# Turning all outputs back on VectorE, and issuing SyncE's transfers in program order

## The chip, the cores and the metric

The kernel runs on one core of a Trainium2 chip. The metric is the device time of one execution in microseconds, as the median of several runs. The core has five engines that run their own instruction streams in order: PE (TensorE, matrix multiply), DVE (VectorE), ACT (ScalarE), POOL (GpSimd) and SP (SyncE, which here only starts transfers). They wait for each other through semaphores.

## The reference, cut to what matters

Two blocks follow each other. The first is attention where each row keeps only its 32 highest scores; the second mixes along the sequence with a low-rank matrix and then runs a two-layer network over the channels.

```python
def _attn_ref(q, k, v):                      # (8, 8, 576, 64) each
    top_k = 32
    scores = scale * np.matmul(q, k.transpose(0, 1, 3, 2))
    kth = np.partition(scores, -top_k, axis=-1)[..., -top_k:-top_k + 1]
    scores = np.where(scores >= kth, scores, -1000000000.0)
    scores = scores - np.max(scores, axis=-1, keepdims=True)
    attn = np.exp(scores)
    attn = attn / (np.sum(attn, axis=-1, keepdims=True) + 1e-09)
    return np.matmul(attn, v)

def _moe_ref(x, U, V, w_ch1, w_ch2):         # x: (8, 576, 512); rank 32; 512 -> 2048 -> 512
    h = x.transpose(0, 2, 1) @ U @ V
    u = x + h.transpose(0, 2, 1)
    ch = np.maximum(u @ w_ch1, 0.0) @ w_ch2
    return u + ch
```

## The kernel before

The work is cut into 32 pairs of heads (four pairs to a batch) and each pair into five row chunks `t`: four of 128 rows, for both heads, and one of 64 rows of both heads together. One row chunk is one step. DVE finds the top 32 of each row with MAX8 and MATCH_REPLACE8, four and three times per head.

PE, ACT, DVE and POOL run their instructions in the order in which the program states them; SP's order is left to the scheduler:

```python
ctx.enter_context(tc.manual_schedule(engines={PE, ACT, DVE, POOL}))
```

PE needs the softmax weights transposed. For head 1 of a chunk, DVE turns 32x32 blocks (`y`), SP writes them to HBM (`away`) and reads them back rearranged (`PT`); this is what `blocks` does. PE multiplies `PT` with v a step later, in `values`:

```python
def blocks(g, t):
    ...
    y = attn.tile([P, 4, NT, BLK], F32, tag="y", name="y", bufs=1)
    nc.vector.transpose(y..., E2[:, S + TAIL : 2 * S]...)
    away = dram.tile([P, 4, P], F32, tag="away", name="away")
    for a in range(4):
        nc.sync.dma_start(away[:, a]..., y[a * BLK : (a + 1) * BLK]...)
    nc.sync.dma_start(PT[:, NT : 2 * NT]..., away...)
```

`load(g)` starts the transfers of a pair: for pairs 5 and later 16 for q and k into one buffer `ld`, and five for v into one of three sets of buffers (`va`, `vd`, `vt`). DVE then turns `ld` into `qkT`. While a batch's attention runs, the network of the batch before it is fed to PE in small portions (`fill`), eight times in a step. It works on transposed activations, with 320 and then 256 of the 576 rows at a time. Its result `oT` is therefore transposed and is turned back, in four blocks of 128 channels for each of the two row groups:

```python
def mlp(b):
    ...
    for chunks, (lo, hi) in zip(PARTS, SPAN):        # 320 rows, then 256 rows
        w = hi - lo
        ...                                          # first layer: 16 x 4 matmuls, Relu on ACT
                if f == 3 and late:
                    late.pop()()
        for c in range(NC):
            po = ps_m.tile([P, C], F32, tag="mm", name="mm")
            for f in range(NF):
                nc.tensor.matmul(po[:, 0:w], lhsT=w2[...], rhs=hTs[f][:, 0:w], ...)
                if f == 9 and late:
                    late.pop()()
                if f < NF - 1:
                    yield w / C
            oT = mlpp.tile([P, WIDE], F32, tag="oT", name="oT")
            if b == B - 1:
                nc.vector.tensor_tensor(oT[:, 0:w], uT[:, c, lo:hi], po[:, 0:w], ALU.add)
            else:
                nc.scalar.copy(oT[:, 0:w], po[:, 0:w])
                nc.gpsimd.tensor_tensor(oT[:, 0:w], oT[:, 0:w], uT[:, c, lo:hi], ALU.add)
            late.append(turned_back(b, chunks, lo, c, oT))
            yield w / C
    late.pop()()
```

So a block is turned back ten matmuls into the next block, except the last one of a batch, which is turned back at once. There are two ways to do it. The last batch goes through DVE in 32x32 blocks, with transfers that put the blocks in place; the others go through PE, PSUM and ACT:

```python
def turned_back(b, chunks, lo, c, oT):
    def run():
        cs = slice(c * P, (c + 1) * P)
        if b == B - 1 and (lo, c) != (SPAN[1][0], NC - 1):
            w = sum(rows(t) for t in chunks)
            ob = mlpp.tile([P, 3 * P], F32, tag="ob", name="ob", bufs=2)
            nc.vector.transpose(ob[:, 0:w], oT[:, 0:w])                       # L631
            for a in range(4):
                ...
                for t in chunks[0:2]:
                    nc.sync.dma_start(out[...], ba[...])                      # L636
                if NT in chunks:
                    nc.sync.dma_start(out[...], ba[...])                      # L641
            return
        tp = ps_t.tile([P, 3, P], F32, tag="tp", name="tp")
        for i, t in enumerate(chunks):
            nc.tensor.transpose(tp[...], oT[...], ident)                      # L649
        ob = mlpp.tile([P, 3, P], F32, tag="ob", name="ob", bufs=2)
        nc.scalar.copy(ob[:, 0:2], tp[:, 0:2, :])                             # L651
        if NT in chunks:
            nc.scalar.copy(ob[0:TAIL, 2], tp[0:TAIL, 2, :])                   # L653
        nc.sync.dma_start(out[...], ob[:, 0:2])                               # L655
        if NT in chunks:
            nc.sync.dma_start(out[...], ob[0:TAIL, 2])                        # L660
    return run
```

## Time and profile before

| | |
|---|---|
| time, median of 3 runs | 1765.89 us (1764.58 to 1766.87) |
| span of the profiled run | 1765.1 us |
| transposes of oT on PE (L649) | 142, own duration 273 ns (median) |
| copies to ob on ACT (L651, L653) | 57 of 373 ns and 28 of 259 ns |
| transposes of oT on DVE (L631) | 7 of 483 ns (mean) |
| transfers of results, SP (L655, L660) | 57 and 28 |
| transfers of results, SP (L636, L641) | 56 and 16 |
| time in which the 16 DMA engines moved q1's packets | 26.0% |

A line number such as L631 names the line of the kernel that made an instruction. Names such as `oT` or `PT<-away` are those of the program's buffers, written as output<-input. PEld is the load of a matmul's stationary operand. "Busy" of PE is the time covered by its records; the records of neighbouring matmuls overlap, so an instruction's own duration is not what it adds. In "A <- B" A is the waiting instruction and B the one that released it; SPq is SP's queue of transfers.

### The profile page before, as it was taken

What the parts mean: (1) busy time and instruction counts of PE and PEld (TensorE: products, weight loads), DVE (VectorE), ACT (ScalarE), POOL (GpSimd) and SP (SyncE); (2) the same over time, 40 slices, a digit from 0 to 9 for tenths busy, and PEclk for the clock granted to TensorE, in tenths of its full rate; (3) what the DMA queues carried; (4) which work ended last, traced back from release to release, by engine and by line L of the source; (5) the groups of instructions that cost most, each with busy time, mean ns of one, the idle gap of its engine ahead of it and who ended that gap; (6) DMA issues with size and microseconds to landing.
All of it is one profiled execution on the core that took longest, in us unless ns stands there. A gap on an engine that the chain in (4) does not pass through costs nothing.

```text
span 1765.1 us, 28989 instructions
## 1 busy us (share of the span) xinstructions
PE 1670.0 (95%) x9851; PEld 1259.5 (71%) x9851; DVE 1540.3 (87%) x3106; ACT 1026.2 (58%) x2682; POOL 846.4 (48%) x591
## 2 busy tenths in 40 slices
PE   4576889999999999999999999999999999999999
PEld 2444556777777877788777877788777877788677
DVE  7999989999999999999999999999999999994000
ACT  4778787655655665565656556565656656564100
POOL 4777677445545454444444454545354554543000
PEclk7677799999999999999999999999999999999999
DMA  3232232232223332222223232223233232211010
GB/s 99 84 90 72 81 85 61 51 66 70 66 59 76 72 72 64 67 66 66 61 62 81 66 72 63 70 61 70 58 68 80 64 76 56 56 45 45 4 15 13
DMA packets 275829, 112.79 MB, mean 64 GB/s; under 512 B 173920, under 2 KB 260192, under 8 KB 275680
## 3 DMA queue, kind: packets, MB, share of 16 engines
q1 hardware_dynamic: 274624, 110.68, 26.0%
q8 instruction: 77, 1.26, 0.3%
q14 instruction: 72, 0.59, 0.1%
q10 hardware_dynamic: 1056, 0.26, 0.1%
HBM read 74.15 MB, written 36.70 MB: 63 GB/s over the span
## 4 chain that ended last, share of the span: by engine, by line
PE 78%; DVE 13%; POOL 4%; ACT 3%; issue 1%; DMA 1%; SPq 0%; POOLq 0%; DVEq 0%
PE mm L582 26%; PE mm L601 25%; PE sc L333 7%; PE O L513 6%; DVE rr L396 6%; DVE m L400 5%; PE tp L475 3%; DVE first L385 2%; PE sc L320 2%; PE O L499 2%; PE up L557 1%; PE O L509 1%; POOL E L403 1%; PE up L559 1%; PE tp L649 1%
## 5 line engine op out<-in xcount | busy, mean ns | idle before, releaser
L400 DVE MAX8 m<-rr 128x8 f32<-128x576 f32 x864 | 614.3, 747 | 5.5
L601 PE MATMUL mm<-hT,w 128*128 128x256 f32 (+1 forms) x2048 | 547.4, 410 | 0.0
L582 PE MATMUL mm<-uT,w 128*128 128x256 f32 (+1 forms) x2048 | 541.1, 410 | 0.8 <-ACT hT L594 0.8
L403 POOL TENSOR_SCALAR E<-Ssb,m 128x576 f32<-128x576 f32 x127 | 280.9, 2212 | 366.2 <-DVE m L400 346.1
L582 PEld LDWEIGHTS mm<-uT,w 128*128 128x128 f32 x2048 | 371.7, 190 | 114.7 <-issue 26.0
L601 PEld LDWEIGHTS mm<-hT,w 128*128 128x128 f32 x2048 | 368.5, 190 | 106.6 <-issue 22.5
L396 DVE MATCH_REPLACE8 rr<-m,rr 128x576 f32<-128x576 f32 x576 | 423.2, 741 | 0.0
L422 POOL TENSOR_TENSOR Ssb<-Ssb,E 128x576 f32<-128x576 f32 x159 | 224.8, 1414 | 147.6 <-ACT E L421 147.6
L594 ACT ACTIVATE hT<-mm 128x320 f32<-128x320 f32 (+1 forms) x256 | 105.0, 410 | 243.8 <-PE mm L582 243.3
L351 ACT ACTIVATE E<-Ssb,nmax 128x576 f32<-128x576 f32 x288 | 223.0, 776 | 37.3 <-POOL Ssb L404 28.1
L385 DVE MAX8 first<-Ssb 128x8 f32<-128x576 f32 x288 | 203.7, 743 | 38.5 <-ACT Ssb L346 37.8
L396 DVE MATCH_REPLACE8 rr<-first,Ssb 128x576 f32<-128x576 f32 x288 | 211.7, 742 | 0.0
L404 POOL TENSOR_TENSOR Ssb<-Ssb,E 128x576 f32<-128x576 f32 x127 | 179.1, 1410 | 10.6
L333 PE MATMUL sc<-qkT 64*128 64x288 f32 x1024 | 170.7, 454 | 6.3 <-ACT Ssb L344 5.2
L513 PE MATMUL O<-PT,va 128*64 128x128 f32 x2048 | 145.4, 285 | 2.0 <-DMA PT<-away 2.0
L475 PE MATMUL tp<-ident,E 128*128 128x128 f32 x736 | 116.0, 284 | 31.5 <-ACT XT L522 11.6
L476 ACT COPY PT<-tp 128x512 f32<-128x512 f32 x184 | 106.4, 585 | 58.0 <-PE tp L475 55.4
L475 PEld LDWEIGHTS tp<-ident,E 128*128 128x128 f32 x736 | 92.5, 146 | 63.2 <-ACT XT L522 13.4
L513 PEld LDWEIGHTS O<-PT,va 128*64 128x64 f32 x2048 | 113.6, 140 | 18.5 <-DMA PT<-away 2.2
L421 ACT ACTIVATE E<-Ssb,least 128x576 f32<-128x576 f32 x159 | 123.3, 776 | 5.2
L333 PEld LDWEIGHTS sc<-qkT 64*128 64x128 f32 x1024 | 93.2, 197 | 44.6 <-issue 14.0
L614 DVE TENSOR_TENSOR oT<-uT,mm 128x320 f32<-128x320 f32 (+1 forms) x8 | 3.6, 454 | 137.1 <-PE mm L601 137.1
(81 smaller groups left out, 1576.4 us busy)
## 6 DMA issues: line engine op xcount, KB each, us to landing
away<-y SPq DMA_DIRECT2D x416, 64.0 KB, 1.8
PT<-away SPq DMA_DIRECT2D x104, 256.0 KB, 2.7
raw<-in_moe_w_ch_dram SPq DMA_DIRECT2D x32, 512.0 KB, 3.8
va<-in_v_dram SPq DMA_DIRECT2D x64, 128.0 KB, 2.2
out_dram<-ob SPq DMA_DIRECT2D x57, 128.0 KB, 2.1
ld<-in_q_dram SPq DMA_DIRECT2D x108, 64.0 KB, 2.4
ld<-in_k_dram SPq DMA_DIRECT2D x108, 64.0 KB, 2.3
ld<-in_q_dram SPq DMA_DIRECT2D x108, 8.0 KB, 2.1
```

Source lines behind the costliest of these rows:

```text
L333: nc.tensor.matmul(sc[:, h, 0:HALF], lhsT=qkT[half(h), 0, cols(t)], rhs=qkT[half(h), 1, i * HALF : (i + 1) * HALF], start=True, stop=True,)
L351: nc.scalar.activation(E, chunk, AF.Exp, bias=nmax, scale=SCALE, accum_out=total)
L385: nc.vector.max(ms[c], curs[c])
L396: nc.vector.match_replace(nxt, ms[c], curs[c], NEG)
L400: nc.vector.max(ms[c], curs[c])
L403: nc.gpsimd.tensor_scalar(Es[c], chunks[c], ms[c][:, 7:8], NEG, ALU.is_lt, ALU.mult)
L404: nc.gpsimd.tensor_tensor(chunks[c], chunks[c], Es[c], ALU.add)
L422: nc.gpsimd.tensor_tensor(chunks[c], chunks[c], Es[c], ALU.subtract)
L475: nc.tensor.transpose(tp[:, j, :], E2[:, a : a + P], ident)
L513: nc.tensor.matmul(O[half(h)], lhsT=va[:, h, j, :], rhs=PB[:, j] if h and shared(g, t) else PT[:, NT * h + j], start=False, stop=(j == NT ...
L582: nc.tensor.matmul(ph[:, 0:w], lhsT=w1[:, cc, f * P : (f + 1) * P], rhs=uT[:, cc, lo:hi], start=(cc == 0), stop=(cc == NC - 1),)
L601: nc.tensor.matmul(po[:, 0:w], lhsT=w2[:, f, c * P : (c + 1) * P], rhs=hTs[f][:, 0:w], start=(f == 0), stop=(f == NF - 1),)
```

## The change

The results of all batches but for one block of the last take the way through DVE, which frees PE and ACT of that work. With it come many more and smaller transfers (eight or twelve in place of one or two per block), and SP is put under the program's order as well, so that its transfers are issued as the program states them.

```diff
-    DVE, POOL = mybir.EngineType.DVE, mybir.EngineType.Pool
+    DVE, POOL, SP = mybir.EngineType.DVE, mybir.EngineType.Pool, mybir.EngineType.SP
...
-    ctx.enter_context(tc.manual_schedule(engines={PE, ACT, DVE, POOL}))
+    ctx.enter_context(tc.manual_schedule(engines={PE, ACT, DVE, POOL, SP}))
...
         def run():
             cs = slice(c * P, (c + 1) * P)
-            if b == B - 1 and (lo, c) != (SPAN[1][0], NC - 1):
+            if (b, lo, c) != (B - 1, SPAN[1][0], NC - 1):
 
                 w = sum(rows(t) for t in chunks)
                 ob = mlpp.tile([P, 3 * P], F32, tag="ob", name="ob", bufs=2)
```

## The prediction

> **What bounds the kernel now.** I read the page first, then the busy time by stretches, then the chain of work in one stretch, then who waited for whom. The engine totals look like two near-equal engines:

> ```profile
> PE 1670.0 (95%) x9851; PEld 1259.5 (71%) x9851; DVE 1540.3 (87%) x3106; ACT 1026.2 (58%) x2682; POOL 846.4 (48%) x591
> PE 78%; DVE 13%; POOL 4%; ACT 3%; issue 1%; DMA 1%; SPq 0%; POOLq 0%; DVEq 0%
> ```

> The second line, the shares of the chain that ended last, says PE. The busy time by stretches (columns: stretch, its length, then PE, PEld, DVE, ACT, POOL) says where:

> ```profile
> 400.00:450.00 50.00, 48.49 (x319) 38.11 (x317) 49.19 (x99) 30.03 (x81) 25.27 (x18) 1.00 0.30 71
> ...
> 700.00:750.00 50.00, 50.00 (x296) 35.89 (x292) 48.57 (x99) 28.10 (x76) 25.57 (x18) 1.00 0.29 70
> 750.00:800.00 50.00, 50.00 (x324) 41.07 (x324) 47.63 (x96) 31.32 (x87) 22.63 (x15) 1.00 0.29 66
> ```

> Until about 440 us the vector engine sets the pace (49.2 of 50). From there PE never stops, but DVE is close behind (47.6 to 48.6 of 50), so there is little room to give it work. One pair of heads takes 50.0 us, a batch of four pairs 200.1 us. From 1616 us on only the last batch's MLP is left and DVE is nearly idle.

> What one transpose costs PE is read from the chain, not from its own duration (columns: start, us, what):

> ```profile
> 1115.44 0.33 PE tp L649 x3
> ...
> 1130.42 0.33 PE tp L649 x3
> ```

> Its own record is 273 ns, but the next matmul starts 0.11 us later. That is the price of a removed one. Last, the waits of SP and of PE (who, for whom, us, times, longest):

> ```profile
> SPq L453 <- DVE y L447: 333.3, 103, 13.9
> SPq L273 <- PE O L499: 117.1, 13, 9.4
> SPq L276 <- PE O L509: 114.7, 26, 12.4
> ...
> PE tp L649 <- POOL oT L617: 2.8, 2, 1.5
> ```

> SP sits at a transfer whose buffer PE has not freed (L273, L276: v fetched too early in the scheduler's order), but nobody suffers: PE waited only 2.0 us for PT<-away.

> [...] So the block grid must be undone by the transfers, and no PSUM copy is needed; the last batch does just that here (0.51 us for 128x320, 0.45 for 128x256). [...] 0.43 us to issue, 1.5 us to landing, for the last batch's output pieces. [...] The new pieces have 128 B; those of the last batch land in 1.5 us[...].

> **The change, part by part.** (1) PE loses the transposes of seven batches: per batch 4x3 + 4x2 = 20, so 140, at 0.11 us = 15.2 us. Of these 120 lie after 440 us, in the PE-bound part: 13.0 us. With them go PE's waits for POOL's oT, 2.8 us. Together 15.8 us gained.

> (2) ACT loses 56 copies of 0.37 and 28 of 0.26 us: 28 us, on an engine busy 58%. No gain of its own after 440 us.

> (3) DVE gets 56 transposes. Neighbours on DVE overlap by about 0.08 us (two MAX8 of 0.74 take 1.41), so they cost 0.43 and 0.37 us: 1.7 us in a pair of heads that emits four wide ones. DVE's 47.8 us of work per pair becomes 49.5, PE's 50.0 becomes about 49.5. Before 440 us DVE is the bound, and the eight transposes there cost 3.2 us nearly in full.

> (4) The DVE queue is in order, so its transpose waits in place for POOL's oT. The orders of both built kernels are the same on PE, DVE and POOL but for what is removed and inserted. So for each new transpose I take from the trace before when oT was ready and when DVE passed that place. In seven of eight per batch oT is ready 3 to 8 us earlier: no wait. The eighth, the last column block of a batch, is turned back at once, without the ten matmuls of delay the others have: oT was ready at 1040.18, DVE passed at 1035.64. DVE will stand 4.5 us there, in each of five steady batches, and 2.9 us in the first (before 440 us, where it counts in full).

> (5) What this costs PE. The stalled DVE is to make y 2.7 us later on, and y goes out to HBM and back as PT. Before: y ends 1039.05, four issues 1.76, landing 1.8, PT issued and landed 2.7, so about 1045.6 with the waits, and PE uses it at 1049.05. After: DVE resumes at 1040.2, the transpose ends 1040.6, y ends 1044.0; SP needs 8 x 0.47 = 3.8 us for the output pieces first and is free at 1044.5; then 1.8 + 1.8 + 0.4 + 2.7 gives 1051.1. PE stops 2 us. In the next step y comes at 1053.7 to 1054.4, PT at 1061.0, PE wants it (2 us late) at 1060.0: another 1 us. Then DVE's usual idle time at the one-chunk step (1.2 and 1.0 us) takes up the rest. Total 3 us per steady batch.

> (6) SP. In program order the 21 loads of the next pair (0.62 us each, 13 us) are issued in one block, with the output pieces behind: 12 x 0.47 = 5.6 us for a wide block, 3.8 for a narrow one, in place of one or two issues. In the pair with wide blocks SP has 13 + 4 x 4.2 + 22.6 = 52 us of work for 50 us, but the blocks lie over some 55 us. By hand, step after step, y finds SP busy for up to 2.4 us, and PT's margin of 1.5 to 4.4 us takes nearly all of it: 0.6 us of PE per batch. In the narrow pair (from about 810 us) the loads end at 824.6, the two blocks behind them at 832.2, while y is done at 828.1: PT lands 6.7 us after 832.2, at 838.9, and PE wants it at 838.6: about 0.5 us. The waits of L273 and L276 vanish, without gain.

> Sum: 1765.9 - 15.8 (PE) + 3.2 + 2.9 - 1 (before 440 us; the 1 is my guess for the freed ACT, whose copies lie in the chain there) + 5 x 3.0 (DVE's stall) + 6 x 0.6 + 5 x 0.5 (SP) = 1776. Several of these delays may hide behind each other, so I take **1773 us**, 0.4% slower.

> **Rivals.** *PE's relief comes through.* If the lead that DVE has over PE takes up the 4.5 us, all that is left is the gain: 1750 us, 0.9% faster. For it: PE waits almost nowhere before. Against: the margins of PT are 1.5 to 4.4 us, less than the delay. More than 1% cannot come of it, for PE has no other idle time to win. *SP becomes the bound.* If the output pieces take longer to issue or land among the other traffic than in the quiet tail, or the loads come too late for DVE's transpose into qkT (after the fourth wide block SP is free at 767.5; 16 loads of q and k take 10.4 us to issue and 2.4 to land, so 780.3, and DVE wants them at 780.30), each step loses one or two us: 8 us per batch, 1805 us or more. For it: SP is almost full in a wide pair. Against: the 16 DMA engines are busy 29% there. *DVE becomes the bound.* 47.8 + 0.8 on average + 1.1 (stall) + 0.4 of small gaps = 50.1 us per pair against 50.0: about 1769 us, the same as my number to the eye.

> **Range and chances.** The gain is bounded by 18 us; the losses are small delays that each could be double. So 1755 to 1800 us. Faster by over 2% would need 35 us that PE does not have: 0.02. Slower by over 2% needs SP's rival: 0.11. Within 2%: 0.87.

> **What will show it.** Right: PE's busy time about 38 us lower (140 x 0.27), but its share of steady stretches below 100%; a wait of DVE's L631 for oT L617, six times, about 4.5 us; waits of PE O L513 for PT<-away of some 20 us in all, up from 2.0; L636 and L641 issues of 0.43 us. Wrong if PE is again at 50.0 of 50 (then 1750), if L631 waits little, if qkT waits for a load, or if away and PT take over 1 us longer to land than 1.8 and 2.7 us.

## The result, and the profile after

The changed kernel takes **1792.32 us** (median of 4 runs, 1790.93 to 1793.99) beside 1766.38 us for the kernel before on the same chip (4 runs, 1764.58 to 1766.91). The ratio is **1.0149, with a 95% interval of 1.0131 to 1.0167**: 1.5% slower. The time lies in the predicted range of 1755 to 1800 us, 19 us above the predicted 1773.

The engine totals and the shares of the chain that ended last, of the kernel after:

```profile
PE 1665.0 (93%) x9711; PEld 1249.7 (70%) x9711; DVE 1560.3 (87%) x3162; ACT 1005.8 (56%) x2598; POOL 846.4 (47%) x591
PE 64%; DVE 19%; DMA 5%; SPq 5%; ACT 3%; POOL 3%; issue 2%; DVEq 0%; POOLq 0%
```

The totals hardly move: 140 PE instructions are gone and PE's busy time falls by 5 us only. The chain tells more: PE's share falls from 78 to 64%, and SP's queue, which had 0%, now holds 5%, with another 5% (before: 1%) for transfers under way.

The busy time by stretches (columns as before: stretch, its length, PE, PEld, DVE, ACT, POOL, then the clock that PE was granted, the share of DMA time, GB/s), after:

```profile
400.00:450.00 50.00, 48.20 (x299) 37.69 (x298) 46.46 (x97) 25.50 (x70) 22.86 (x17) 1.00 0.32 68
700.00:750.00 50.00, 50.00 (x295) 35.73 (x293) 48.67 (x101) 27.63 (x73) 24.95 (x17) 1.00 0.31 67
750.00:800.00 50.00, 48.97 (x301) 38.98 (x299) 48.35 (x98) 29.95 (x80) 23.24 (x15) 1.00 0.32 69
840.00:860.00 20.00, 17.83 (x97) 13.21 (x96) 17.26 (x35) 7.67 (x20) 10.50 (x8) 0.91 0.31 63
1000.00:1250.00 250.00, 245.12 (x1475) 188.59 (x1474) 236.05 (x480) 141.16 (x374) 115.50 (x78) 0.99 0.30 66
```

The same view of the kernel before, for the last stretch:

```profile
1000.00:1250.00 250.00, 249.76 (x1531) 192.82 (x1527) 238.83 (x481) 148.69 (x397) 121.24 (x82) 1.00 0.29 68
```

PE no longer fills the part that it bounded. The holes are local: none between 700 and 750 us, 1 us between 750 and 800, over 2 us in the 20 us from 840. DVE is not fuller either (236 of 250, before 239). So no engine has become the bound; something stands between them. The waits (who, for whom, us, times, longest) name it:

```profile
DVE ob L631 <- POOL oT L617: 41.1, 9, 10.5
PEld O L513 <- DMA PT<-away: 29.7, 21, 3.2
PE O L513 <- DMA PT<-away: 24.6, 18, 3.0
```

The last of these lines in the kernel before:

```profile
PE O L513 <- DMA PT<-away: 2.0, 1, 2.0
```

PE's wait for PT, the attention weights that travel to HBM and back, rises from 2.0 to 24.6 us. DVE's new transpose L631 waits for oT: six of these nine waits last 2.74 to 2.95 us and are the last column block of each batch; the other three, up to 10.5 us, are at the end of attention, where DVE has little else.

How such a stop of PE comes about can be followed around 845 us. First SP (start, us, what; a row with x16 is sixteen issues in a row, with the waits between them):

```profile
835.79 0.63 SPq L277 DMA_DIRECT2D vt<-in_v_dram  x1
836.53 8.89 SPq L636 DMA_DIRECT2D out_dram<-ob  x16
845.51 1.83 SPq L453 DMA_DIRECT2D away<-y  x4
848.80 0.34 SPq L457 DMA_DIRECT2D PT<-away  x1
849.23 7.58 SPq L636 DMA_DIRECT2D out_dram<-ob  x16
856.91 1.82 SPq L453 DMA_DIRECT2D away<-y  x4
```

Then DVE in the same microseconds (the bracket is the wait in front of a row):

```profile
838.18 0.69 DVE L447 STREAM_TRANSPOSE y<-E 128x512 f32<-128x512 f32 x1
...
850.05 0.45 DVE L631 STREAM_TRANSPOSE ob<-oT 128x256 f32<-128x256 f32 x1 [2.74 <-POOL oT L617]
...
853.17 0.69 DVE L447 STREAM_TRANSPOSE y<-E 128x512 f32<-128x512 f32 x1
```

And PE:

```profile
851.56 1.09 PE L513 MATMUL O<-PT,va 128*64 128x128 f32 x14 [2.17 <-DMA PT<-away]
852.58 1.88 PE L333 MATMUL sc<-qkT 64*128 64x288 f32 x8
854.39 3.97 PE L582 MATMUL mm<-uT,w 128*128 128x320 f32 x10
```

DVE finishes y at 838.87. SP is then two microseconds into sixteen output pieces, which in turn had stood behind 21 loads, and sends y at 845.51, 6.6 us later. PT is issued at 848.80 and lands at 851.5; PE stood from 849.39. The next y, ready at 853.86, waits until 856.91 behind the next sixteen pieces. Note also that DVE's own wait (847.3 to 850.05) comes after the late y: this stop is SP's, not DVE's.

The transfers themselves are no slower: `away`, PT and 16 KB pieces took a median of 1.8, 2.7 and 1.5 us from issue to landing before as well. The transfer part of the page of the kernel after (transfer, count, KB each, median us from issue to landing):

```profile
away<-y SPq DMA_DIRECT2D x416, 64.0 KB, 1.8
PT<-away SPq DMA_DIRECT2D x104, 256.0 KB, 2.7
...
out_dram<-ob SPq DMA_DIRECT2D x504, 16.0 KB, 1.5
```

### The profile page after: what moved, and what is told of

Its sections match the earlier page's. It is cut to its first block, busy times and chain, and to the rows that moved or that the text cites. A ratio compares the mean times of both kernels' runs of the same rounds, so it can differ in the third digit from the quotient of the medians.

```text
span 1789.1 us, 29116 instructions
## 1 busy us (share of the span) xinstructions
PE 1665.0 (93%) x9711; PEld 1249.7 (70%) x9711; DVE 1560.3 (87%) x3162; ACT 1005.8 (56%) x2598; POOL 846.4 (47%) x591
## 4 chain that ended last, share of the span: by engine, by line
PE 64%; DVE 19%; DMA 5%; SPq 5%; ACT 3%; POOL 3%; issue 2%; DVEq 0%; POOLq 0%
PE mm L582 24%; PE mm L601 19%; DVE rr L396 8%; DVE m L400 7%; PE sc L333 6%; PE O L513 5%; DVE first L385 3%; PE tp L475 3%; DMA PT<-away 2%; PE sc L320 2%; SPq L636 2%; PE O L499 1%; DMA away<-y 1%; PE up L557 1%; PE O L509 1%
## 5 line engine op out<-in xcount | busy, mean ns | idle before, releaser
L582 PE MATMUL mm<-uT,w 128*128 128x256 f32 (+1 forms) x2048 | 542.8, 412 | 2.4 <-ACT hT L594 2.4
L582 PEld LDWEIGHTS mm<-uT,w 128*128 128x128 f32 x2048 | 373.3, 191 | 120.0 <-issue 29.8
L333 PE MATMUL sc<-qkT 64*128 64x288 f32 x1024 | 170.9, 455 | 8.8 <-ACT Ssb L344 7.8
L513 PE MATMUL O<-PT,va 128*64 128x128 f32 x2048 | 154.9, 286 | 24.7 <-DMA PT<-away 24.6
L513 PEld LDWEIGHTS O<-PT,va 128*64 128x64 f32 x2048 | 118.1, 140 | 45.9 <-DMA PT<-away 29.7
L333 PEld LDWEIGHTS sc<-qkT 64*128 64x128 f32 x1024 | 93.4, 198 | 47.6 <-issue 15.5
```

The source lines that it names most:

```text
L333: nc.tensor.matmul(sc[:, h, 0:HALF], lhsT=qkT[half(h), 0, cols(t)], rhs=qkT[half(h), 1, i * HALF : (i + 1) * HALF], start=True, stop=True,)
L513: nc.tensor.matmul(O[half(h)], lhsT=va[:, h, j, :], rhs=PB[:, j] if h and shared(g, t) else PT[:, NT * h + j], start=False, stop=(j == NT ...
L582: nc.tensor.matmul(ph[:, 0:w], lhsT=w1[:, cc, f * P : (f + 1) * P], rhs=uT[:, cc, lo:hi], start=(cc == 0), stop=(cc == NC - 1),)
```

## The experiments

Two suspects: SP's queue in order (with 560 more output pieces in it, seven batches x 4 x (12 + 8), where the kernel before sent each block in one or two transfers), and DVE's wait in place for oT. Rivals: the program order on SP alone; the block of 21 loads; ACT's or DVE's changed load. All times are medians, and the ratios are to the kernel before on the same chip (1765.85 to 1766.4 us). "Stops" is PE's lost time between 440 and 1610 us, counted from the start times of the same matmuls in the trace before and in the trace of the run, with the time of the removed transposes taken out; it includes small shifts. In the kernel after it is 36.3 us. Stops and waits are those of the one profiled execution of each kernel. The pairs of heads in which blocks of 320 rows are turned are called wide below, those with blocks of 256 rows narrow.

| run | what it is | us | ratio, 95% interval | stops, us | PE's wait for PT, us |
|---|---|---|---|---|---|
| after | the change | 1792.32 | 1.0149, 1.0131 to 1.0167 | 36.3 | 24.6 |
| e1_sp_order_only | SP in program order, results turned by PE | 1766.30 | 1.0001, 0.9992 to 1.0009 | 0.9 | 1.6 |
| e2_dve_only | results turned by DVE, SP scheduled | 1781.34 | 1.0092, 1.0076 to 1.0107 | 30.8 | 16.3 |
| e3_no_out_dma | after, pieces of 7 batches not sent | 1768.57 | 1.0013, 1.0006 to 1.0020 | 18.3 | 6.1 |
| e4_late_last | after, last block turned later | 1776.79 | 1.0058, 1.0042 to 1.0075 | 22.4 | 19.7 |
| e7_late_no_out_dma | both of these | 1752.90 | 0.9925, 0.9910 to 0.9939 | 3.8 | 2.4 |
| e6_behind | after, pieces held behind y | 1802.36 | 1.0206, 1.0189 to 1.0223 | 50.1 | 14.3 |
| e8_late_behind | e4 and e6 | 1784.39 | 1.0102, 1.0087 to 1.0117 | 32.4 | 12.4 |
| e10_late_behind_free | e8, but at once in steps without y | 1769.68 | 1.0023, 1.0013 to 1.0033 | 18.6 | 13.5 |
| e11_late_behind_v | e10, v loaded three steps later | 1781.30 | 1.0085, 1.0068 to 1.0102 | 30.2 | 20.2 |
| e12_v_later | after, v loaded three steps later | 1794.98 | 1.0164, 1.0149 to 1.0179 | 41.6 | 24.4 |
| e9_late_scheduled | e4, SP scheduled | 1761.42 | 0.9973, 0.9963 to 0.9984 | 5.0 | 7.3 |
| e13_placed | e4, pieces and v put by hand | 1760.82 | 0.9971, 0.9959 to 0.9984 | 8.7 | 8.1 |

### The two halves of the change

e1_sp_order_only keeps the program order on SP and lets PE turn the results of seven batches, as before:

```diff
-            if (b, lo, c) != (B - 1, SPAN[1][0], NC - 1):
+            if b == B - 1 and (lo, c) != (SPAN[1][0], NC - 1):
```

> SP issues in program order, but the results of batches 0 to 6 go back through PE as before. Theory S (the transfers of y wait in SP's queue behind the block of 21 loads and behind 8 or 12 output pieces) says the loads alone are not enough, because y comes 15 us after they start and they take 13: 1766 us, within 3 us of the kernel before, PE waiting under 5 us for PT<-away. Theory D (DVE stands in its queue for oT of a batch's last block, and that delays PE) says the same, as that instruction is not there. A third, O (the order alone does it), says over 1775 us.

It takes the same time as before, within 0.1%. Its waits:

```profile
SPq L453 <- DVE y L447: 423.2, 93, 14.5
SPq L457 <- DMA away<-y: 142.1, 204, 2.6
```

The waits of SP for v's buffers (L273 and L276, 232 us in the kernel before) are gone, and SP waits longer for y instead. The block of 21 loads is in this queue as well. Neither costs anything: the order alone is not the cause.

e2_dve_only is the other half, all results turned by DVE and SP left to the scheduler:

```diff
-    ctx.enter_context(tc.manual_schedule(engines={PE, ACT, DVE, POOL, SP}))
+    ctx.enter_context(tc.manual_schedule(engines={PE, ACT, DVE, POOL}))
```

> Results of all batches turned by DVE with the many small pieces, but SP's order left to the scheduler. Theory S: the scheduler mixes loads, pieces and y's transfers, so y waits less for a whole block, but the number of issues is the same: 1775 to 1790 us. Theory D: the wait of DVE for oT is the same 2.7 us, so the time stays at 1788 to 1795 us. If the order was set because the scheduler places the pieces badly, over 1800 us.

0.9% slower than before, and 11 us faster than the whole change. (Its profiled execution took 1786.77 us, 5 us above the median, so its 30.8 us of stops are on the high side.) So turning on DVE, with its waits and pieces, is what costs, and once the pieces exist the program order makes it 11 us worse. The order is harmless alone and harmful with the pieces.

### The two causes, one at a time

e3_no_out_dma leaves out the transfers of the results of batches 0 to 6 (those results are not written); DVE's transposes and its waits for oT stay:

```diff
-                for a in range(4):
+                for a in range(4) if b == B - 1 else ():
```

> The changed kernel without the output transfers of batches 0 to 6 (DVE still turns every block; the results of seven batches are not written). Theory S: away goes out at once, PE's waits for PT<-away fall from 24.6 us to under 6, time 1752 to 1762 us. Theory D: the DVE wait is still there and still delays y by 2.7 us: waits of 15 us or more, time 1780 to 1790 us.

```profile
DVE ob L631 <- POOL oT L617: 41.2, 9, 10.5
PE O L513 <- DMA PT<-away: 6.1, 12, 1.6
```

1768.57 us: the pieces cost 23.8 us. The time lies between the ranges of the two theories: DVE's waits are all still there, and they cost something too.

e4_late_last keeps the pieces and takes DVE's wait away: the last block of a batch stays in the list and is turned back after the next batch's fourth column block, as the other blocks are turned after ten matmuls of delay:

```diff
+    late = []
+
     def mlp(b):
...
-        late = []
...
-        late.pop()()
+        if b == B - 1:
+            late.pop()()
```

> The changed kernel, but the last block of a batch is turned back four matmul columns into the next batch's network instead of at once, so oT is long ready when DVE gets there. Theory D: the six waits of 2.7 us are gone and the delays with them, time 1765 to 1772 us. Theory S: the first stop of PE in each batch, caused by loads and two blocks of pieces ahead of y, stays, and only the second goes: 1780 to 1788 us.

```profile
DVE ob L633 <- POOL oT L618: 24.5, 3, 10.5
PE O L513 <- DMA PT<-away: 19.7, 16, 3.0
```

(Line numbers shift with an edit: L633 and L618 here are L631 and L617 above.) The six short waits of DVE are gone and the three at the end stay; the time falls by 15.5 us, and lies between the two ranges again. The edit also takes the last block's eight pieces away from the y that followed them; the next run separates this from the wait.

The two runs also say which stop belongs to which cause. Near the last blocks of a batch the change made two groups of stops in five batches: one where PE uses PT in the first step of a pair of heads (in the trace before at 638.9, 839.0, 1039.1, 1239.2 and 1439.4 us), one in the step after it (648.7, 848.8, 1048.9, 1249.0 and 1449.2 us). With the kernel after, the first group lost 1.2, 2.3, 1.5, 2.3 and 2.9 us, the second 2.4, 0, 3.0, 1.5 and 0. In e4 the first group is still there (0.9, 2.1, 1.5, 3.0 and 2.0) and the second is gone. In e3 the first group is gone, and a second is left (0.4 to 1.7 us). The first comes with the pieces in SP's queue. The second needs DVE's wait, and the pieces make it larger (6.9 us in all, 3.4 in e3). The first batch has a stop of 2.4 us right behind DVE's first wait, where the trace before stands at 448 us; in e3 it is 3.2 us, in e4 and e7 it is gone, so it is DVE's too.

e7_late_no_out_dma makes both edits (again the results of seven batches are not written):

> Later last block and no output transfers for batches 0 to 6 (results of seven batches not written). The two causes taken away wholly; what is left is PE's relief and DVE's added work. If they add: 1750 to 1754 us. If DVE's added work is a bound of its own, 1760 us or more, with PE waiting for E or PT although SP is free.

```profile
PE O L513 <- DMA PT<-away: 2.4, 4, 0.9
```

```profile
1000.00:1250.00 250.00, 249.86 (x1514) 191.60 (x1513) 244.15 (x495) 146.73 (x386) 122.47 (x83) 1.00 0.28 63
```

1752.90 us. The two causes add: 1792.3 - 23.8 - 15.5 = 1753.0. No pieces of the seven batches are sent in e3 or e7, so the 15.7 us between these two are DVE's wait alone; and the pieces cost 23.9 us without the wait (e4 to e7), 23.8 with it. PE is full again, and the kernel is 0.75% faster than before, which is most of PE's relief. Only 3.8 us of stops are left.

### Can the pieces be sent without the cost?

e6_behind holds the pieces of a step and sends them behind y, away and PT of that step (the edit, with the piece loops unchanged inside `send`):

```diff
+                while len(sends) > 1:
+                    sends.pop(0)()
                 ob = mlpp.tile([P, 3 * P], F32, tag="ob", name="ob", bufs=2)
...
+                if b == B - 1:
+                    send()
+                else:
+                    sends.append(send)
...
             blocks(*divmod(n - 1, CH))
+        while sends and t:
+            sends.pop(0)()
```

> The changed kernel, but the output pieces of batches 0 to 6 are held back and issued right after the y, away, PT transfers of their step, so y never stands behind more than the loads. If the harm of the pieces is only their place in SP's queue, this is as good as leaving them out: 1766 to 1771 us, with the waits of DVE for oT (2.7 us each) still there. If it is their number or their load on the transfer engines, the time stays over 1780 us.

```profile
DVE ob L635 <- DMA out_dram<-ob: 28.9, 8, 5.2
```

A miss: 1802.36 us, slower than the change. PE's wait for PT fell to 14.3 us, but a wait that was not there before took its place: `ob` has two buffers, and a block whose pieces are held keeps its buffer, so DVE stands in place until they have landed. e8_late_behind joins this with e4's later last block:

> Both cures at once: pieces issued behind y's transfers, and the last block of a batch turned back later. If the two causes add (leaving the pieces out took 24 us, the later last block 15 us), 1792 - 24 - 15 = 1753 us, 0.7% faster than the kernel before, and PE waits for PT<-away under 4 us. If they are the same delay seen twice, 1766 us.

```profile
841.80 0.45 DVE L637 STREAM_TRANSPOSE ob<-oT 128x256 f32<-128x256 f32 x1 [4.97 <-DMA out_dram<-ob]
```

Also a miss (1784.39 us), for the same reason: five such waits, 20.8 us in all. e10_late_behind_free holds pieces only where a step has a y:

```diff
-        while sends and t:
+        while sends:
             sends.pop(0)()
```

> As e8, but in a step without y the pieces go out at once, so that a buffer ob is free when DVE turns the next block but one. If e8 was slow only because DVE waited for the transfers that read ob (20.8 us in all), this is at 1755 to 1760 us and that wait is gone. If holding pieces behind y harms in another way, 1770 us or more.

The wait for `ob` is gone, and 14.7 us with it, but 1769.68 us is still 17 us above e7. What is left lies behind a pair with wide blocks, where 13 us of loads and 5.6 us of held pieces fall between two y: at the end of one wide pair, loads and pieces held SP from 764.82 to 784.77 us, while y was done at 778.48. The obvious next step was to spread the loads. e11_late_behind_v issues v's five transfers three steps later:

```diff
+    def load_v(g):
...
+                if not blocked(g + 1):
+                    load_v(g + 1)
+            if t == 3 and g + 1 < NP and blocked(g + 1):
+                load_v(g + 1)
```

> As e10, and the five transfers of v of the next pair are issued three steps later, so the block of loads takes 10 us of SP in place of 13. Theory S: y of the following step finds SP free a little earlier, 1 to 4 us better than e10: 1752 to 1757 us. If what is left is DVE's work, no difference.

A miss. SP's queue in this run:

```profile
754.86 0.43 SPq L276 DMA_DIRECT2D va<-in_v_dram  x1
...
757.07 0.64 SPq L280 DMA_DIRECT2D vt<-in_v_dram  x1
757.81 2.00 SPq L456 DMA_DIRECT2D away<-y  x4
```

y was ready at 754.86, and the five v issues, which got to the head of the queue at that moment, held it for 3 us. e12_v_later does the same move in the changed kernel, without the other edits:

> The changed kernel with only v's five transfers moved three steps later. Theory S (loads and two blocks of pieces stand before y in the narrow pair): y of that step goes out 2.7 us earlier, so PE's first stop of each batch of 1.2 to 2.3 us is mostly gone: 1780 to 1786 us. If the pieces alone matter, not what stands before them, under 3 us of gain.

```profile
767.72 1.97 PE L516 MATMUL O<-PT,va 128*64 128x128 f32 x14 [1.98 <-DMA PT<-away]
```

The first group of stops is gone in all five batches, as hoped, which confirms that loads and pieces together made it: around the ends of the batches PE loses 6 us less than in the changed kernel. But the moved issues delayed other y, as at 767.72 us, and between the ends PE loses 11 us more. The time did not fall (1794.98 us). In this queue the moved transfers moved the delay with them.

### Two versions that are faster than before

e9_late_scheduled leaves SP to the scheduler and keeps the later last block:

> Later last block, and SP's order left to the scheduler. If the causes add: 1781 - 15 = 1766 us, as the kernel before; the scheduler's order would then cost some 10 us more than pieces behind y. If the scheduler's order already avoided the delay, 1755 us.

The time, 1761.42 us, lies between the two figures: the scheduler's order avoids most of the pieces' delay, but not all (5.0 us of stops).

e13_placed keeps the program order, but places by what the traces above showed: pieces go at once, except those that arise in the first step before its y, which go behind it; v's loads go behind the first y of the pair (behind the second where `g % NPAIR` is 0, a narrow pair):

```diff
+                if held:
+                    sends.append(send)
+                else:
+                    send()
...
+            if t == (3 if g % NPAIR == 0 else 2) and g + 1 < NP and blocked(g + 1):
+                load_v(g + 1)
...
+        if away and t == 1:
+            held.append(n)
...
             blocks(*divmod(n - 1, CH))
+        held.clear()
+        while sends:
+            sends.pop(0)()
```

> The changed kernel with a later last block and SP's issues placed by counting: in the pair with narrow blocks the pieces of the second block go behind the first y, the five transfers of v behind the first y (behind the second in the narrow pair), all else at once as the program states it. The work between two y is then at most what fits before the next y by SP's issue times. Theory S and D add: PE waits for PT<-away under 6 us, time 1752 to 1760 us, faster than the kernel before. If SP's order does not decide, about as e4: 1777 us.

```profile
PE O L516 <- DMA PT<-away: 8.1, 9, 3.0
```

```profile
1000.00:1250.00 250.00, 249.34 (x1513) 191.72 (x1512) 244.16 (x496) 145.63 (x384) 121.31 (x82) 1.00 0.31 68
```

1760.82 us is just outside the expected range, and PE's wait of 8.1 us just over the 6. The two versions, 1761.42 and 1760.82 us, are both 0.3% faster than before, with intervals that end below 1, and not told apart from each other. They win back 31 of the 39 us that the pieces and the wait cost. 8 us are left to e7, which sends no pieces; whether a third `ob` buffer or fewer, larger pieces would win these too was not tried.

## Why the prediction was right in kind and short in size

Its sum gave +10 us (1776, taken down to 1773); measured are +25.9. The runs with and without the wait and the pieces divide this by the terms of the sum:

| part | in the sum | measured |
|---|---|---|
| PE's relief, DVE's transposes, freed ACT: -15.8 + 3.2 - 1 | -13.6 | -13.5 (e7 beside the kernel before) |
| DVE's wait, steps 4 and 5: 2.9 + 5 x 3.0 | 17.9 | 15.5 (e4 to after), 15.7 (e7 to e3) |
| SP, step 6: 6 x 0.6 + 5 x 0.5 | 6.1 | 23.8 (e3 to after), 23.9 (e7 to e4) |

- **PE's relief** (steps 1 and 2): real, as e7 shows. The 142 L649 instructions took 15.9 us from one start to the next in the trace before. That the line of the table agrees so well is in part luck: in e7 the stretch before 440 us became 1.9 us shorter, where the sum had 2.2 longer, the part up to 1610 us 8.7 shorter in place of 15.8, and the end 2.4 shorter, which was not in the sum. The sign that was to show the relief was wrong: busy time fell by 5 us, not 38. In e7, where hardly a stop is left, it fell by 16: the removed records overlapped their neighbours, and with the stops the slow matmuls (below) fill some of it again.
- **Before 440 us** (3.2 + 2.9 - 1 = 5.1): 4.7 measured, with the relief taken out, and this is luck. Without the pieces it is 0.7 (e3) or 0.5 (e7), so 4 of the 4.7 us came with the pieces, for which the sum had nothing here. The first wait of DVE ended at 441.24 us, and its cost lies just behind 440.
- **DVE's wait** (steps 4 and 5): foreseen at the right instruction and six times, at 4.5 us each and 2.9 in the first batch. It was 2.74 to 2.95 us: beside the trace before, DVE came to the place near 1050 us 14.7 us later, and oT was ready 12.9 us later. What it cost was nearly right. In e3, where it stands alone, each of the five steady batches loses 2.5 to 2.7 us over two steps (3.0 in the sum), and the first 5.2 (2.9).
- **SP** (step 6): **this is the term that failed**, by 18 us. Between e3 and the kernel after, 4.0 us lie before 440 us (nothing in the sum), 11.2 around the ends of the batches (2.5) and 6.8 in the other steps (3.6). In the narrow pair followed above, the step had the loads end 3.5 us before y was done (824.6 and 828.1); it was 2.4 us (836.42 and 838.87). The sixteen pieces took 8.89 us in place of 7.6. So y stood 6.6 us, not 4.1. Its way back as PT was quicker than worked out (6.0 us, not 6.7), and PE, which was to stop 0.3 us (838.9 against 838.6, taken as 0.5), stopped 2.17. The step subtracted a margin from a delay of nearly its size, so an error of 2 us in the delay became the whole stop. The first group of stops came to 10.2 us, with 2.5 in the sum.
- **Not in the sum**: matmuls at a granted clock of 0.50 after a stop, about 6.7 us (last section), part of the measured figures above; and about 5 of the 36.3 us of stops, small shifts of mostly under 0.2 us each, not traced to a cause.

Taking 3 us off the sum because delays "may hide behind each other" went the wrong way as well. Delays did hide (in two of five batches the second stop is missing: PE, late from the first, found PT there), but stops also bred more time.

The rivals: "PE's relief comes through" is what e7 shows once both causes are out (1752.9; 1750 was said). "SP becomes the bound" named the right queue, with twice the size: 8 us per batch, measured 23.8 for the batches together, about 4 each. Its extreme form, loads late for qkT, showed once, for 0.6 us. "DVE becomes the bound" was wrong; DVE had 236 us of work in 250. Issuing was again not small beside the transfer: the time is lost in SP's sixteen issues (8.89 and 7.58 us above), not in the 1.5 us of landing.

## What to carry to other kernels

When one queue carries both a round trip that the bound engine needs and bulk transfers that nobody waits for, count the issues that can stand ahead of the round trip, and compare their time with its margin: here sixteen issues of 0.47 us against a margin of 1.5 to 4.4 us. Look at each place where an engine in order consumes something fresh (here the last block of a batch, six waits of 2.74 to 2.95 us) and let it consume it later; that one move was worth 15.5 us. Before holding a transfer back, count the buffers that its source keeps (two of `ob`, and 28.9 us of DVE's waits for them in e6_behind), and before moving one, look at what then stands behind it (in e12_v_later 6 us won at the ends of the batches and 11 us lost between them).

## What was not expected of the hardware

Four stops of PE in the kernel after cost more than their length. After the 2.17 us stop shown above, eight L333 matmuls (scores), which start in pairs, took 1.88 us, the last two pairs 0.47 us apart; undisturbed, in the kernel before, they take 1.24 us, with 0.24 us there:

```profile
858.85 1.24 PE L333 MATMUL sc<-qkT 64*128 64x288 f32 x8
```

L582 (first layer) went from 0.27 to 0.53 us apart, and then, some 5 us after PE resumed, back. Behind the stops at 450, 850, 1064 and 1461 us slow matmuls added 1.6, 1.7, 1.6 and 1.7 us. The stops of 2.25 us before 659.21 and of 2.14 us before 1260.59 added nothing of the kind. The recorded clock differs between the two kinds. In the traces before and after it changes only on a grid of 3.41 us, and these are stretches of that grid in the kernel after (PE's busy time stands behind the length, the granted clock third from the end):

```profile
849.64:853.05 3.41, 1.49 (x18) 1.27 (x20) 3.00 (x7) 0.61 (x3) 0.38 (x1) 1.00 0.47 108
853.05:856.46 3.41, 3.41 (x12) 1.94 (x9) 3.41 (x8) 1.44 (x4) 0.33 (x1) 0.50 0.24 37
856.46:859.87 3.41, 3.41 (x14) 2.32 (x14) 3.41 (x8) 1.30 (x3) 3.33 (x3) 1.00 0.41 89
...
655.08:658.49 3.41, 1.88 (x9) 1.14 (x7) 3.41 (x8) 2.04 (x5) 2.52 (x2) 1.00 0.35 98
658.49:661.91 3.42, 2.70 (x24) 1.80 (x25) 3.42 (x9) 0.72 (x3) 0.00 (x0) 1.00 0.15 43
```
